# First block of a two-layer MLP behind gated attention: fp32 products from unsplit weights, decoding shared differently between VectorE and ScalarE, and weights loaded on the SyncE queue

## The chip, the cores and the metric

One core of a Trainium2 chip. The metric is the device time of one execution in microseconds (us). The kernel before takes 895.98 us (median of 3 runs, 895.06 to 896.11).

## The reference, cut to what matters

```
x = attn(q, k, v, f_logit)          # per head: state = f * state + k v^T ; y = q state
x = relu(x @ w_in) ** 2 @ w_out     # layer 0, 3072 tokens, 384 -> 2048 -> 384
out = elu(x @ w2_in) @ w2_out       # layer 1, same sizes
```

The weights arrive as 64-bit floats: each is two 32-bit words, and the kernel itself puts sign, exponent and mantissa together into a 32-bit float (it decodes them).

## The kernel before, in words

Tokens stand in 24 groups of 128 (g0 to g23); four groups make a block of 512 tokens, so there are six blocks per layer. The hidden size 2048 is cut into 16 slices of 128, numbered f. For a block i and a slice f, `up(i, f)` multiplies the block's input with the slice of w_in into a PSUM tile ph (9 matmuls: input and weights each split into a high and a low part in TensorE's reduced 32-bit format fp32r; products high-high, low-high, high-low). `between(i, f)` makes gg = relu(ph)^2 and its own parts gh and gl. `down(i, f)` multiplies with the slice of w_out into three PSUM tiles y (3 x 3 matmuls). The order is written out by hand: a table of steps (`START`) for the first four groups, then slots u = 2, 3, ...: the planned steps of the slot, up of unit u, down of unit u - 2, between of unit u. The first block is slots 0 to 17. In this text U3 is up(0, 3), D3 is down(0, 3), U1,0 is up(1, 0).

A weight slice f of layer 0 goes through these steps. `load_raw`: one DMA of 768 KB; slices 0 to 2 on SyncE's queue (SP), the others on ScalarE's. `decode`: one pass of ScalarE (L54) and three of VectorE (L56, L59, L60) over 128x768. `split`: the high part by ScalarE (L370), the low part by VectorE (L371). For f < 8 (`WHOLE`) only the w_in half is split then; the w_out half stays as it was decoded for the first block, whose D0 to D7 are done in plain fp32 (one matmul of two passes instead of three matmuls: 6 passes for a down), and `split_rest` splits it in slots 10 to 13.

Groups g4 to g7 are the attention of the second block and are worked in the slots of the first: load_qk, a_gate, a_decay (VectorE scans), a_scale, a_keys (transpose tp), a_near (TensorE), a_far, a_out (TensorE, tile o). Between a_far and a_out ScalarE makes `seen`, a small copy from o for which a_out waits. After a_out ScalarE copies o to x1 in four pieces (L293), and six small DMAs on SP (L296) move rows of x1 into place. Engines work through their own instructions in the order written, SP too: a DMA behind one that waits is not issued before it.

Of the kernel before, what the change touches and what calls it, by code (L numbers as in the profile page):

```python
# [32 lines left out]

START = """f0 q0 f1 I q1 M v0 f2 v1 f3 g0 q2 d0 q3 c0 g1 v2 d1 s0 r0 c1 r1 t0 g2 k0 m0 g3 s1 t1 y0 d2 c2 h0 v3 k1
# [4 lines left out]
NEAR = dict(zip(range(B, NG), (4, 6, 9, 11, 19, 21, 23, 25, *range(28, 4 * NG - 23, 4))))  # L39
ORDER = np.r_[64:128, 63:-1:-1]  # L40
# [21 lines left out]

def chunked(ctx, tc, ff, qk, vk, vz, wraw, mask, ident, flag, out):
# [79 lines left out]
    def a_gate(g):  # L143

        f = st[g]["ff"]
        A.activation(f, f, AF.Tanh, scale=0.5)
        if g < B:
            A.activation(f, f, AF.Copy, scale=0.5, bias=0.5)
        else:
            G.tensor_scalar(out=f, in0=f, scalar1=0.5, scalar2=0.5, op0=ALU.mult, op1=ALU.add)  # L150

    def a_decay(g):


        a, f = ds[g % 2], st[g]["ff"]
        V.memset(lim[:, ::65], 1.0)
        V.tensor_tensor_scan(out=a[:, 0, 0:520], data0=f[:, 0:520], data1=lim[:, 0:520], initial=1.0, op0=ALU.mult, op1=ALU.max)  # L157
        V.reciprocal(out=lim[:, 65::65], in_=a[:, 0, 64::65])
# [12 lines left out]

    def a_scale(g):

        a = ds[g % 2]
        for o, first, apart in ((0, 66, 456), (1, 0, 588)):
            y = st[g]["qk"[o]].rearrange("r (p h l) -> r p h l", h=2, l=64)
            z = bass.AP(a.tensor, a.offset + first, [a.ap[0], [130, NP], [apart, 2], [1, 64]])

            E = G if o == 0 and 0 < g < B else V
            E.tensor_tensor(out=y, in0=y, in1=z, op=ALU.mult)  # L180
# [173 lines left out]
    def whole(layer, f):  # L354
        return layer == 0 and f < WHOLE

    def decode_weights(layer, f):

        if whole(layer, f):
# [13 lines left out]
    def split_weights(layer, f):  # L373

        pool, tag = (two, "raw") if layer else (wpool, "w")
        t = pool.tile([128, 2, 2, DM], F32R, tag=tag, name=f"w{layer}_{f}")
        if layer == 0:
            wt[layer, f] = t
        if whole(layer, f):
            split(t[:, :, 0:1], raws[layer, f][:, :DM].bitcast(F32))  # L380
            return
# [1 line left out]
        if layer:
            nc.sync.dma_start(out=wst[f], in_=t.bitcast(F32))

    def split_rest(f):
        split(wt[0, f][:, :, 1:2], raws.pop((0, f))[:, DM:].bitcast(F32))

# [360 lines left out]
```

## Time and profile before

| | |
|---|---|
| median of 3 runs | 895.98 us |
| profiled execution: own time / span | 894.93 us / 893.0 us |
| busy: TensorE (PE) / VectorE (DVE) / ScalarE (ACT) / GpSimd (POOL) | 97% / 63% / 50% / 31% |
| chain that ended last: PE / DVE / DMA | 88% / 5% / 2% |
| granted TensorE clock, mean | 0.996 |

The span runs from the first to the last instruction; the rest of the execution's own time lies around it. Busy shares are means over stages with different limits: over the first 110 us VectorE is busy more than 90% of most stretches, afterwards TensorE is.

### The profile page before, as it was taken

What the parts mean: (1) busy time and instruction counts of PE and PEld (TensorE: products, weight loads), DVE (VectorE), ACT (ScalarE), POOL (GpSimd) and SP (SyncE); (2) the same over time, 40 slices, a digit from 0 to 9 for tenths busy, and PEclk for the clock granted to TensorE, in tenths of its full rate; (3) what the DMA queues carried; (4) which work ended last, traced back from release to release, by engine and by line L of the source; (5) the groups of instructions that cost most, each with busy time, mean ns of one, the idle gap of its engine ahead of it and who ended that gap; (6) DMA issues with size and microseconds to landing.
All of it is one profiled execution on the core that took longest, in us unless ns stands there. A gap on an engine that the chain in (4) does not pass through costs nothing.

```text
span 893.0 us, 15986 instructions
## 1 busy us (share of the span) xinstructions
PE 867.9 (97%) x6273; PEld 704.3 (79%) x6273; DVE 564.8 (63%) x858; ACT 443.6 (50%) x797; POOL 279.9 (31%) x245
## 2 busy tenths in 40 slices
PE   6699999999999999999999999999999999999997
PEld 4555778888888888888888888888888888888886
DVE  8799987778777877844331565564555555655543
ACT  4456863545555445544544444544444544544443
POOL 3101036343333332323333232323232323333331
PEclk9999999999999999999999999999999999999999
DMA  9555342324354433523587400100100100100001
GB/s 268 190 167 186 121 118 74 113 87 151 129 160 153 162 114 116 181 87 109 183 310 249 166 12 1 60 12 1 60 13 0 60 12 1 60 12 11 26 1 39
DMA packets 34210, 88.66 MB, mean 99 GB/s; under 512 B 5552, under 2 KB 11056, under 8 KB 34128
## 3 DMA queue, kind: packets, MB, share of 16 engines
q1 hardware_dynamic: 32112, 77.22, 26.6%
q10 hardware_dynamic: 2016, 10.36, 3.4%
q8 instruction: 50, 0.82, 0.4%
q14 instruction: 32, 0.26, 0.1%
HBM read 64.55 MB, written 22.02 MB: 97 GB/s over the span
## 4 chain that ended last, share of the span: by engine, by line
PE 88%; DVE 5%; DMA 2%; ACT 1%; issue 1%; SPq 1%; POOL 0%; ACTq 0%; DVEq 0%
PE ph L413 42%; PE y L477 41%; DMA ff<-ff 1%; PE o L270 1%; PE o L285 1%; PE tp L186 1%; DVE ds L157 1%; PE sk_a L209 1%; SPq L296 1%; DVE dec L59 1%; DVE w L371 1%; PE sk_a L218 1%; DVE pair L60 0%; DVE pair L59 0%; DMA vk<-vk 0%
## 5 line engine op out<-in xcount | busy, mean ns | idle before, releaser
L460 POOL TENSOR_TENSOR gl<-gg,gh 128x512 fp32r<-128x512 f32 x175 | 234.4, 1340 | 457.1 <-PE ph L413 189.5
L477 PE MATMUL y<-gh,wf 128*128 128x512 f32 (+1 forms) x582 | 177.8, 387 | 0.0
L446 DVE SCALAR_TENSOR_TENSOR t<-r,t 128x512 f32<-128x512 f32 (+1 forms) x97 | 71.4, 736 | 154.5 <-ACT r L445 154.2
L477 PE MATMUL y<-gh,w 128*128 128x512 f32 x528 | 162.5, 389 | 0.0
L413 PE MATMUL ph<-xh,w 128*128 128x512 f32 x576 | 155.1, 403 | 4.6 <-ACT w L370 3.8
L442 ACT ACTIVATE r<-ph 128x512 f32<-128x512 f32 (+1 forms) x97 | 57.8, 596 | 181.5 <-PE ph L413 176.6
L413 PE MATMUL ph<-xh,wf 128*128 128x512 f32 (+1 forms) x582 | 146.4, 387 | 0.0
L413 PEld LDWEIGHTS ph<-xh,w 128*128 128x128 f32 x576 | 105.1, 189 | 29.6 <-ACT w L370 4.2
L477 PEld LDWEIGHTS y<-gh,wf 128*128 128x128 f32 x582 | 108.8, 188 | 22.3
L413 PEld LDWEIGHTS ph<-xh,wf 128*128 128x128 f32 x582 | 108.6, 188 | 22.3
L477 PEld LDWEIGHTS y<-gh,w 128*128 128x128 f32 x528 | 99.1, 188 | 20.6
L477 PE MATMUL y<-gl,wf 128*128 128x512 f32 (+1 forms) x291 | 112.6, 387 | 0.0
L477 PE MATMUL y<-gl,w 128*128 128x512 f32 x264 | 102.7, 389 | 0.0
L434 ACT ACTIVATE r<-ph 128x512 f32<-128x512 f32 x88 | 52.2, 593 | 95.7 <-PE ph L413 87.4
L413 PE MATMUL ph<-xl,w 128*128 128x512 f32 x288 | 81.3, 390 | 1.0 <-DVE xl L322 1.0
L413 PE MATMUL ph<-xl,wf 128*128 128x512 f32 (+1 forms) x291 | 81.1, 387 | 0.0
L440 DVE TENSOR_TENSOR gh<-r 128x512 fp32r<-128x512 f32 x64 | 44.0, 688 | 54.9 <-ACT r L434 51.2
L447 DVE SCALAR_TENSOR_TENSOR gg<-ph,t 128x512 f32<-128x512 f32 (+1 forms) x97 | 66.6, 687 | 10.4 <-DVE t L446 0.5
L413 PEld LDWEIGHTS ph<-xl,w 128*128 128x128 f32 x288 | 54.3, 189 | 13.1 <-DVE xl L322 1.4
L477 PEld LDWEIGHTS y<-gl,wf 128*128 128x128 f32 x291 | 54.6, 188 | 11.1
L413 PEld LDWEIGHTS ph<-xl,wf 128*128 128x128 f32 x291 | 54.4, 188 | 11.1
L444 ACT ACTIVATE t<-r 128x512 f32<-128x512 f32 (+1 forms) x97 | 61.0, 629 | 3.1
(101 smaller groups left out, 1013.9 us busy)
## 6 DMA issues: line engine op xcount, KB each, us to landing
raw<-wraw SPq DMA_DIRECT2D x19, 768.0 KB, 6.3
wst<-w SPq DMA_DIRECT2D x16, 768.0 KB, 4.3
wf<-wst SPq DMA_DIRECT2D x16, 768.0 KB, 5.2
raw<-wraw ACTq DMA_DIRECT2D x13, 768.0 KB, 4.3
ff<-ff SPq DMA_DIRECT2D x22, 227.9 KB, 4.5
k<-qk SPq DMA_DIRECT2D x22, 224.0 KB, 4.4
q<-qk SPq DMA_DIRECT2D x22, 224.0 KB, 4.8
x2d<-yo SPq DMA_DIRECT2D x18, 256.0 KB, 2.9
```

The costliest lines, as they stand in the source:

```text
L59: V.scalar_tensor_tensor(out=out, in0=hi, scalar=0x80000000, in1=out, op0=ALU.bitwise_and, op1=ALU.bitwise_or)
L157: V.tensor_tensor_scan(out=a[:, 0, 0:520], data0=f[:, 0:520], data1=lim[:, 0:520], initial=1.0, op0=ALU.mult, op1=ALU.max)
L186: PE.transpose(tp[:, p, 0:ROWS], k[:, p], idt[:ROWS, :ROWS])
L413: PE.matmul(ph, w[:, a, 0, 128 * k:128 * k + 128], b[:, k, c], start=(m == 0), stop=(m == len(todo) - 1))
L434: A.activation(r[:, c], ph, AF.Relu)
L440: V.tensor_tensor(out=gh[:, c], in0=r[:, c], in1=r[:, c], op=ALU.mult)
L442: A.activation(r[:, c], ph, AF.Relu, scale=-1.0)
L444: A.activation(t[:, c], r[:, c], AF.Tanh, scale=-0.5)
L446: V.scalar_tensor_tensor(out=t[:, c], in0=r[:, c], scalar=1.0, in1=t[:, c], op0=ALU.add, op1=ALU.mult)
L447: V.scalar_tensor_tensor(out=gg[:, c], in0=ph, scalar=0.0, in1=t[:, c], op0=ALU.max, op1=ALU.add)
L460: G.tensor_tensor(out=gl, in0=gg, in1=gh, op=ALU.subtract)
L477: PE.matmul(yp_[i][m][:, c], w[:, 128 * m:128 * m + 128], b[:, c], start=(f == 0 and n_ == 0), stop=(f == NF - 1 and n_ == 2), skip_group_ ...
```

## The change: what it does

- The raw weights of layer 0 are all loaded on SP's queue. Slices 2 to 9 go to buffers of the large pool `wpool` and are loaded four slots ahead (before: three, in two buffers); slices 10 to 15 three slots ahead, in the two old buffers.
- Decoding is divided into `begin` (two ScalarE passes: the old one, and one that reads a byte of each weight and writes the three low bits as a word) and `finish` (two VectorE passes; L56 is gone).
- U0 to U2 are done in plain fp32, with an unsplit copy `x` of the block's input (`a_whole`, four small ScalarE copies). All of D0 to D15 are done in plain fp32. `between` of the first block makes neither gh nor gl.
- `store_weights` copies the decoded half (for f < 3 the whole slice) by a DMA on SP into the slice's final tile; `split_rest` splits it there in place in slots 14 to 31.
- a_scale of g3 multiplies q on VectorE, not GpSimd; gate and first scan of g0 are done in two halves; `START` and four places of the attention (`NEAR`) are rearranged: a_near of g4 and g5 is in slots 5 and 7 (before 4 and 6).

```diff
-START = """... t1 y0 d2 c2 h0 v3 k1
-m1 s2 d3 v4 t2 y1 c3 k2 m2 s3 h1 w0 t3 l0 y2 k3 m3 W0 r2 h2 q4 w1 y3 f4 l1
-l2 h3 l3 W1 g4 r3 w2 U0 B0 L0 W2 d4 U1 B1 L1 w3 r4 T f5"""
+START = """... t1 y0 d2 c2
+x0 r2 k1 m1 s2 d3 f4 q4 t2 y1 c3 b0 k2 s3 m2 x1 r3 t3 b1 y2 x2 m3 y3 k3 w0 h0 h1 r4 x3 w1 U0 B0 b2 C0 w2 h2 h3
+g4 C1 l0 l1 U1 B1 b3 l2 l3 w3 b4 C2 r5 f5 T"""
-WHOLE = 8
-NEAR = dict(zip(range(B, NG), (4, 6, 9, 11, 19, ...
+DIRECT = 3
+EARLY = 10
+NEAR = dict(zip(range(B, NG), (5, 7, 9, 11, 19, ...
+def begin(nc, raw, out):
+    words = raw.bitcast(U32).rearrange("p (n two) -> p n two", two=2)
+    top = raw.bitcast(U8).rearrange("p (n b) -> p n b", b=8)[:, :, 3]
+    hi, lo = words[:, :, 1], words[:, :, 0]
+    nc.scalar.activation(out.bitcast(F32), hi.bitcast(F32), AF.Copy, scale=2.0**-112)
+    nc.scalar.activation(lo, top, AF.Copy, scale=1 / 32, bias=-31 / 64)
+def finish(nc, raw, out):
+    ...
+    V.scalar_tensor_tensor(out=out, in0=out, scalar=3, in1=lo, op0=ALU.logical_shift_left, op1=ALU.bitwise_or)
+    V.scalar_tensor_tensor(out=out, in0=hi, scalar=0x80000000, in1=out, op0=ALU.bitwise_and, op1=ALU.bitwise_or)
+    def a_whole(g):
+        if g == 0:
+            st["x"] = wpool.tile([128, NK, 512], F32, tag="w", name="x")
+        A.activation(st["x"][:, :, 128 * g:128 * g + 128], st[g]["yp"], AF.Copy)
     def load_raw(layer, f):
-        raws[layer, f] = raw = two.tile([128, 2 * DM], I64, tag="raw", name=f"raw{layer}_{f}")
-        (nc.sync if layer or f < 3 else nc.scalar).dma_start(out=raw, in_=wraw[layer, f])
+        pool, tag = (wpool, "w") if layer == 0 and 1 < f < EARLY else (two, "raw")
+        raws[layer, f] = raw = pool.tile([128, 2 * DM], I64, tag=tag, name=f"raw{layer}_{f}")
+        nc.sync.dma_start(out=raw, in_=wraw[layer, f])
+    def store_weights(f):
+        wt[0, f] = t = wpool.tile([128, 2, 2, DM], F32R, tag="w", name=f"w0_{f}")
+        t, b = t.bitcast(F32), decs[f].bitcast(F32)
+        if f < DIRECT:
+            nc.sync.dma_start(out=t[:, 1].rearrange("r i m -> r (i m)"), in_=b)
+        else:
+            nc.sync.dma_start(out=t[:, 1, 1], in_=b[:, DM:])
+    def split_up(f):
+        split(wt[0, f][:, :, 0:1], decs.pop(f)[:, :DM].bitcast(F32))
+    def split_rest(f):
+        t = wt[0, f] if f < DIRECT else wt[0, f][:, :, 1:2]
+        split(t, t[:, 1].rearrange("r i m -> r (i m)").bitcast(F32))
     def up(i, f):
+        if i == 0 and f < DIRECT:
+            ...
+            for k in range(NK):
+                PE.matmul(ph, w[:, 128 * k:128 * k + 128], st["x"][:, k], start=k == 0, stop=k == NK - 1)
     def between(i, f):
-        if i == 0 and f < WHOLE:
+        if i == 0:
     def down(i, f):
-            terms = (raws[0, f][:, DM:].bitcast(F32), gg),
+            terms = (wt[0, f][:, 1, 1].bitcast(F32), gg),
     for f in range(NF):
-        at(f - 3, load_raw, 0, f)
-        at(f - 2, decode_weights, 0, f)
-        at(f - 1, split_weights, 0, f)
-        if f < WHOLE:
-            at(10 + f // 2, split_rest, f)
+        at(f - 1, store_weights, f)
+        if f >= DIRECT:
+            at(f - 1, split_up, f)
+    for f in range(NF):
+        at(f - 3 if f >= EARLY else f - 4, load_raw, 0, f)
+        at(f - 2 if f >= EARLY else f - 3, begin_weights, f)
+        at(f - 2, finish_weights, f)
+        at(f + (NF - 2 if f < DIRECT else NF), split_rest, f)
```

In the order listings below, a row is line, operation, output<-inputs, size; xN counts equal rows that follow each other. SP's queue of before, from the loads of g6 to the copies x1_5 of g5:

```order
L126 DMA k6_614<-qk 112x512
L127 DMA q6_613<-qk 112x512
L296 DMA x1_4_716<-x1_4_716 16x128 x6
L114 DMA ff7_740<-ff 112x521
L140 DMA vk6_771<-vk 128x384
L126 DMA k7_774<-qk 112x512
L127 DMA q7_773<-qk 112x512
L296 DMA x1_5_927<-x1_5_927 16x128 x6
```

The same stretch of SP's queue in the changed kernel (raw0_10 is the raw slice 10 of layer 0, w0_8 the store of slice 8):

```order
L320 DMA x1_4_747<-x1_4_747 16x128 x6
L147 DMA k7_766<-qk 112x512
L148 DMA q7_765<-qk 112x512
L408 DMA w0_8_771<-pair8_614 128x384
L383 DMA raw0_10_777<-wraw 128x768
L161 DMA vk6_803<-vk 128x384
L408 DMA w0_9_813<-pair8_614 128x384
L383 DMA raw0_11_822<-wraw 128x768
L320 DMA x1_5_912<-x1_5_912 16x128 x6
L408 DMA w0_10_930<-dec0_10_817 128x384
L383 DMA raw0_12_939<-wraw 128x768
```

The raw loads of slices 10 and 12 now stand behind the six copies of x1_4 and of x1_5. ScalarE's order of before, slots 7 to 9:

```order
L352 DMA raw0_10_787<-wraw 128x768
L422 ACTIVATE r0_7_802<-ph0_7_0_789 128x512
L423 ACTIVATE gg0_7_803<-r0_7_802 128x512
L231 ACTIVATE kt6_811<-tp6_806 128x448
L370 ACTIVATE w0_9_821<-dec0_9_782 128x768
L54 ACTIVATE dec0_10_824<-raw0_10_787 128x768
L352 DMA raw0_11_829<-wraw 128x768
L434 ACTIVATE r0_8_846<-ph0_8_0_831 128x512
L435 ACTIVATE gg0_8_847<-r0_8_846 128x512
L438 ACTIVATE gh0_8_844<-r0_8_846 128x512
L316 ACTIVATE xh1_852<-x1_4_716 128x3x128
L277 ACTIVATE seen5_874<-o5_0_856 48x4
```

The same slots of ScalarE in the changed kernel:

```order
L474 ACTIVATE r0_7_792<-ph0_7_0_779 128x512
L475 ACTIVATE gg0_7_793<-r0_7_792 128x512
L255 ACTIVATE kt6_801<-tp6_796 128x448
L425 ACTIVATE w0_9_813<-pair8_614 128x384
L70 ACTIVATE dec0_10_817<-raw0_10_777 128x768
L72 ACTIVATE raw0_10_777<-raw0_10_777 128x768
L474 ACTIVATE r0_8_837<-ph0_8_0_824 128x512
L475 ACTIVATE gg0_8_838<-r0_8_837 128x512
L301 ACTIVATE seen5_859<-o5_0_841 48x4
```

The raw loads are gone from ScalarE's queue, the decoding of slice 10 is two passes, and seen5 still stands behind it.

## Rows read from the trace of the kernel before

**Rows 1.** Windows: us, then busy of each engine, PEclk, DMA share, GB/s.

```profile
40.00:41.00 1.00, 1.00 (x3) 0.83 (x3) 0.93 (x1) 0.77 (x2) 0.00 (x0) 0.50 0.02 6
...
90.00:100.00 10.00, 9.71 (x160) 7.91 (x161) 9.79 (x18) 7.83 (x18) 0.00 (x0) 1.00 0.39 120
...
160.00:180.00 20.00, 20.00 (x212) 16.42 (x210) 14.14 (x22) 10.11 (x22) 9.64 (x9) 1.00 0.44 133
```

**Rows 2.** Timeline of TensorE: start us, us, what, count, idle before and releaser.

```profile
30.00 1.65 PE L413 MATMUL ph<-xh,w 128*128 128x512 f32 x6 [0.58 <-ACT xh L316]
...
39.41 3.09 PE L413 MATMUL ph<-xh,w 128*128 128x512 f32 x6 [3.77 <-ACT w L370]
...
63.84 0.66 PE L270 MATMUL o<-q,s 48*48 48x64 f32 x32
...
65.80 1.65 PE L413 MATMUL ph<-xh,w 128*128 128x512 f32 x6
...
78.23 2.74 PE L477 MATMUL y<-gg,pair 128*128 128x512 f32 x6
80.90 0.66 PE L270 MATMUL o<-q,s 48*48 48x64 f32 x32
...
120.76 1.52 PE L413 MATMUL ph<-xh,w 128*128 128x512 f32 x6
...
124.84 1.52 PE L413 MATMUL ph<-xh,w 128*128 128x512 f32 x6
...
128.92 0.55 PE L186 MATMUL tp<-idt,k 112*128 112x112 f32 x4
```

**Rows 3.** Timeline of VectorE, same columns.

```profile
26.51 1.33 DVE L236 COPY_PREDICATED ss<-msk,sc 128x512 f32<-128x512 int32 x2
...
49.74 0.07 DVE L156 MEMSET lim<- 112x9 f32 x1
...
52.64 0.55 DVE L371 TENSOR_TENSOR w<-pair,w 128x384 fp32r<-128x384 f32 x1
53.11 0.55 DVE L56 TENSOR_SCALAR pair<-pair 128x768 uint32<-128x768 uint32 x1
53.70 0.96 DVE L59 SCALAR_TENSOR_TENSOR pair<-raw,pair 128x768 uint32<-128x768 uint32 x1
...
55.57 0.43 DVE L236 COPY_PREDICATED sd<-tri,sk_a 128x256 f32<-128x256 int32 x1
...
57.29 0.68 DVE L180 TENSOR_TENSOR q<-q,ds 112x512 f32<-112x512 f32 x1
```

**Rows 4.** Timeline of ScalarE, same columns.

```profile
46.11 0.90 ACT L54 ACTIVATE pair<-raw 128x768 f32<-128x768 f32 x1
46.91 0.59 ACT L422 ACTIVATE r<-ph 128x512 f32<-128x512 f32 x1
47.52 0.64 ACT L423 ACTIVATE gg<-r 128x512 f32<-128x512 f32 x1
48.06 0.53 ACT L231 ACTIVATE kt<-tp 128x448 f32<-128x448 f32 x1
...
95.61 0.23 ACT L277 ACTIVATE seen<-o 48x4 f32<-48x4 f32 x2
96.59 0.79 ACT L293 ACTIVATE x<-o 48x256 f32<-48x256 f32 x2 [0.75 <-PE o L285]
```

**Rows 5.** Timeline of SP's queue, same columns (SPq: issue of a DMA).

```profile
66.74 3.85 SPq L296 DMA_DIRECT2D x<-x  x6
70.70 0.51 SPq L114 DMA_DIRECT2D ff<-ff  x1
```

**Rows 6.** DMA issues: count, KB, us to landing; window 73:75, then the whole run.

```profile
raw<-wraw ACTq DMA_DIRECT2D x1, 768.0 KB, 5.4
...
raw<-wraw ACTq DMA_DIRECT2D x13, 768.0 KB, 4.3
```

**Rows 7.** Waits, window 0:145: engine and line, for whom, us in total, times, longest.

```profile
PE o L285 <- ACT seen L277: 1.7, 3, 1.2
```

**Rows 8.** Waits of SP's queue, window 0:130, same columns.

```profile
SPq L296 <- ACT x L293: 36.6, 7, 12.7
```

More of the change, by code (lines that the diff above doesn't have):

```diff
@@ L15 @@
 U32 = mybir.dt.uint32
+U8 = mybir.dt.uint8
 I64 = mybir.dt.int64
@@ L31 @@
 BLOCKS = [(layer, sum(n[:i]), n[i]) for layer, n in enumerate(SIZES) for i in range(len(n))]
[L34 to L36 removed]
+START = """f0 q0 f1 I q1 M f2 v0 f3 v1 g0 q2 d0 q3 c0 g1 r0 d1 s0 v2 c1 v3 t0 g2 k0 m0 g3 r1 s1 t1 y0 d2 c2
+x0 r2 k1 m1 s2 d3 f4 q4 t2 y1 c3 b0 k2 s3 m2 x1 r3 t3 b1 y2 x2 m3 y3 k3 w0 h0 h1 r4 x3 w1 U0 B0 b2 C0 w2 h2 h3
+g4 C1 l0 l1 U1 B1 b3 l2 l3 w3 b4 C2 r5 f5 T"""
 STAGED = 27
[L38 to L39 removed]
+DIRECT = 3
+EARLY = 10
+NEAR = dict(zip(range(B, NG), (5, 7, 9, 11, 19, 21, 23, 25, *range(28, 4 * NG - 23, 4))))
 ORDER = np.r_[64:128, 63:-1:-1]
@@ L60, in decode @@
     V.scalar_tensor_tensor(out=out, in0=lo, scalar=29, in1=out, op0=ALU.logical_shift_right, op1=ALU.bitwise_or)
+def begin(nc, raw, out):
[5 more added lines that the diff above has]
+def finish(nc, raw, out):
+    words = raw.bitcast(U32).rearrange("p (n two) -> p n two", two=2)
+    hi, lo = words[:, :, 1], words[:, :, 0]
+    V = nc.vector
+    V.scalar_tensor_tensor(out=out, in0=out, scalar=3, in1=lo, op0=ALU.logical_shift_left, op1=ALU.bitwise_or)
+    V.scalar_tensor_tensor(out=out, in0=hi, scalar=0x80000000, in1=out, op0=ALU.bitwise_and, op1=ALU.bitwise_or)
 def chunked(ctx, tc, ff, qk, vk, vz, wraw, mask, ident, flag, out):
@@ L145, in a_gate @@
         f = st[g]["ff"]
-        A.activation(f, f, AF.Tanh, scale=0.5)
         if g < B:
-            A.activation(f, f, AF.Copy, scale=0.5, bias=0.5)
+            for c in (slice(0, 260), slice(260, 521)) if g == 0 else (slice(0, 521),):
+                A.activation(f[:, c], f[:, c], AF.Tanh, scale=0.5)
+                A.activation(f[:, c], f[:, c], AF.Copy, scale=0.5, bias=0.5)
         else:
+            A.activation(f, f, AF.Tanh, scale=0.5)
             G.tensor_scalar(out=f, in0=f, scalar1=0.5, scalar2=0.5, op0=ALU.mult, op1=ALU.add)
@@ L156, in a_decay @@
         V.memset(lim[:, ::65], 1.0)
-        V.tensor_tensor_scan(out=a[:, 0, 0:520], data0=f[:, 0:520], data1=lim[:, 0:520], initial=1.0, op0=ALU.mult, op1=ALU.max)
+        for c in (slice(0, 260), slice(260, 520)) if g == 0 else (slice(0, 520),):
+            V.tensor_tensor_scan(out=a[:, 0, c], data0=f[:, c], data1=lim[:, c], initial=1.0, op0=ALU.mult, op1=ALU.max)
         V.reciprocal(out=lim[:, 65::65], in_=a[:, 0, 64::65])
@@ L177, in a_scale @@
             z = bass.AP(a.tensor, a.offset + first, [a.ap[0], [130, NP], [apart, 2], [1, 64]])
-            E = G if o == 0 and 0 < g < B else V
+            E = G if o == 0 and 0 < g < B - 1 else V
             E.tensor_tensor(out=y, in0=y, in1=z, op=ALU.mult)
@@ L350, in load_raw, with begin_weights @@
     def load_raw(layer, f):
-        raws[layer, f] = raw = two.tile([128, 2 * DM], I64, tag="raw", name=f"raw{layer}_{f}")
-        (nc.sync if layer or f < 3 else nc.scalar).dma_start(out=raw, in_=wraw[layer, f])
[L354 to L359, printed above, removed]
+        pool, tag = (wpool, "w") if layer == 0 and 1 < f < EARLY else (two, "raw")
+        raws[layer, f] = raw = pool.tile([128, 2 * DM], I64, tag=tag, name=f"raw{layer}_{f}")
+        nc.sync.dma_start(out=raw, in_=wraw[layer, f])
+    decs = {}
+    def begin_weights(f):
+        if f < EARLY:
             if f % 2 == 0:
@@ L363, in decode_weights, with finish_weights @@
         else:
-            b = two.tile([128, 2 * DM], U32, tag="dec", name=f"dec{layer}_{f}")
+            b = two.tile([128, 2 * DM], U32, tag="dec", name=f"dec0_{f}")
+        begin(nc, raws[0, f], b)
+        decs[f] = b
+    def finish_weights(f):
+        finish(nc, raws.pop((0, f)), decs[f])
+    def store_weights(f):
[10 more added lines that the diff above has]
+        split(t, t[:, 1].rearrange("r i m -> r (i m)").bitcast(F32))
+    def decode_weights(layer, f):
+        b = two.tile([128, 2 * DM], U32, tag="dec", name=f"dec{layer}_{f}")
         decode(nc, raws[layer, f], b)
@@ L373, in split_weights @@
     def split_weights(layer, f):
[L375 to L381, printed above, removed]
+        t = two.tile([128, 2, 2, DM], F32R, tag="raw", name=f"w{layer}_{f}")
         split(t, raws.pop((layer, f)).bitcast(F32))
[L383 to L387, printed above, removed]
+        nc.sync.dma_start(out=wst[f], in_=t.bitcast(F32))
     def fetch_weights(f):
@@ L404, in up @@
         layer, t0, n = BLOCKS[i]
+        if i == 0 and f < DIRECT:
+            ph = ps_h.tile([128, n], F32, tag="h", name=f"ph{i}_{f}_0")
+            w = decs[f].bitcast(F32)
+            for k in range(NK):
+                PE.matmul(ph, w[:, 128 * k:128 * k + 128], st["x"][:, k], start=k == 0, stop=k == NK - 1)
+            hs[i, f] = [ph]
+            return
         xh, xl = xr[i]
@@ L478, in down @@
                         yp_[i][m][:, c], w[:, 128 * m:128 * m + 128], b[:, c],
-                        start=(f == 0 and n_ == 0), stop=(f == NF - 1 and n_ == 2),
+                        start=(f == 0 and n_ == 0), stop=(f == NF - 1 and n_ == len(terms) - 1),
                         skip_group_check=i == final[0],
```

8 lines of the change are left out of this document (4 added, 4 removed).

## Prediction

> **What bounds the kernel now.** I read the windows first. In 160 to 180 us TensorE (PE) is busy 20.00 of 20 us and VectorE 14.14 [rows 1], and so it stays to the end: after the first block a microsecond comes off the total only if it comes off TensorE. In 90 to 100 us VectorE is busy 9.79 of 10 [rows 1]. So the first block is the place, and the timeline of TensorE gives its two ends: U0 starts at 30.00, and the last down of the block is over when the transpose at 128.92 starts [rows 2]. All that the change does is priced by what it does to 128.92; the profiled execution's own time is 894.93 us, 1.05 below the median of 895.98.
>
> What is in these 98.9 us? An up and a down of nine fp32r matmuls take 124.84 - 120.76 = 4.08 us, 2.04 each; a down in fp32 takes 2.74 with the tail of its last pass, and 2.67 to the next start [rows 2]: I use 2.6. One far-near-out part of the attention takes 65.80 - 63.84 = 1.96 [rows 2]. With 18 ups at 2.04 (some 0.15 more where one follows attention), 8 downs at 2.6, 8 at 2.04 and some 9.8 us of attention, TensorE has 85 us of work there, and waits for the rest, about 14.
>
> **What goes from VectorE.** L56 is 53.70 - 53.11 = 0.59 [rows 3], 16 times: 9.4 us. Eight subtractions gl of 128x512 go (about 0.6 each, as L180 of that size [rows 3]): 4.8. The low parts of 16 half slices and of three more are moved behind the block, 0.47 each [rows 3]: 8.9. That is 23 us of about 86. What is left per slice is finish, 55.57 - 53.70 = 1.87, and one split, 0.47 [rows 3]. Over two slots, with the scans of one group (52.64 - 49.74 = 2.90), its masks and states (57.29 - 55.57 = 1.72) and q and k (1.2), VectorE has 10.5 us [rows 3], TensorE 2 x (2.04 + 2.6) and about 2.6 of attention, 11.9. So from the fourth slice on VectorE no longer sets the pace.
>
> **What comes to TensorE.** Eight downs and three ups go from 2.04 to 2.6: 11 x 0.56 = 6.2 us, all on the path where nothing waits. An up in fp32 is not in the trace; its passes are those of the fp32 down, between 2.04 and 2.67, so 2.6.
>
> **What comes to ScalarE.** The second pass of begin is not in the trace. Nearest is L54, same 768 columns at the same stride: 46.91 - 46.11 = 0.80 from start to start [rows 4]. Below it lies 0.6 (L422, 512 columns [rows 4]); nothing rules out twice 0.80, if reading bytes or writing words that far apart is slow. I take 0.80, so begin is 1.6. ScalarE's sum over two slots is then 9.6 of 11.9 us (begin 3.2, two high parts 0.9, r and gg 2.3, gate, kt and xh 1.4, seen and x1 1.8); it is not the sum that hurts but the order, below.
>
> **What is hidden.** The stores land long before they are read (three slots, over 13 us, against 4.3 us for a load of four times the size [rows 6]). The late splits (16 in slots 14 to 31, 13 at 0.47 on VectorE and 3 at about 0.9) come to 8.8 us in some 85 us in which VectorE has 30% free [rows 1]: nothing, at most 2 us where they meet scans.
>
> **The walk.** I follow the changed order with these durations.
>
> U0: the masks of group 3 stood behind the first decoding (26.51 [rows 3]) and no longer do, some 1.6 us gained; but ScalarE now makes state, two xh and the last x in front of U0, about 1.1 more. U0 at 29.5, between 28.5 and 30.5 (30.00 before).
>
> U2: begin of slice 2 stands behind r and gg of U0 on ScalarE. U0 ends at 32.2, r and gg take 48.06 - 46.91 = 1.15 [rows 4], begin 1.6, finish 1.87: U2 starts at 36.8. U1 is over at 34.7, TensorE waits 2.1.
>
> U3: VectorE does four xl (0.47 each, as the split) to 38.7, waits for begin of slice 3 (35.0 + xh, gate, r, gg, begin = 39.25), finish to 41.1, then the scans of g4, 2.9, and only then the split: 44.5. TensorE is through U2 and D0 at 42.0 and waits 2.2 in U3, over at 46.4.
>
> Then D1, tp, U4, D2, near, U5, D3, tp, U6, D4, far-near-out: 4 x 2.6, 3 x 2.2 (an up behind attention is some 0.15 longer), two tp at 0.4, near 1.1, 2.0 = 20.9. The attention of g4 is out at 67.3. All slices up to 9 are ready by then.
>
> Slice 10: its raw load stands on SP behind the six copies of x1_4, k7, q7 and a store. ScalarE makes the first two pieces of x1_4 in 0.79 [rows 4], the copies take 3.85, the other issues 0.5 each [rows 5]: issued at 67.3 + 0.8 + 3.85 + 1.5 = 73.45. Slice 10 of before, with loads in flight ahead of it, took 5.4 [rows 6]: landed at 78.85. On ScalarE begin stands in front of r, gg and seen5, and out5 waits for seen5 (such waits are there before: 1.7 us, three times [rows 7]). 78.85 + 1.6 + 1.15 + 0.23 + out 0.5 = 82.35. TensorE is ready for out5 at 78.8: it waits 3.05.
>
> From here it is a loop: x1 0.79, copies 3.85, store 0.5, load 4.3 (median [rows 6]), begin 1.6, r and gg 1.15, seen 0.23, out 0.5: 12.9 us from out5 to out6 and again to out7, against 12.0 and 10.55 of TensorE's own work (U9, D7, tp, U10, D8, attention; U11, D9, U12, D10, far and out). Waits 0.9 and 2.35; out7 ends at 108.15. Behind it stand U13, U14, U15, U1,0, U1,1 and D11 to D15: 2.2 + 4 x 2.04 + 5 x 2.6 = 23.4, so the block ends at 131.5, against 128.92: **2.6 us later**. By the own time 897.5; with the 1.05 us between own time and median, **898.6 us**. In sum: 6.2 of work more on TensorE, waits of 10.6 instead of some 14, and a start 0.5 earlier.
>
> **A rule that would change this.** The issue times above come to little, and SP's x copies did wait before: 36.6 us for ScalarE, up to 12.7 at a time [rows 8]. The Trainium skill (DMA: Bandwidth & Descriptors, Issuing engines are not separate DMA queues) says that issuing DMAs from several engines only saves the time of issuing. By that rule the move of the raw loads from ScalarE's queue to SP costs nothing, which is the first rival below; the trace does not agree here, since what a load loses on SP is not issue time but the wait of what stands ahead of it [rows 8].
>
> **Rivals.**
> 1. Faster: the raw loads of 10, 12 and 14 never hold ScalarE, because SP passes the copies sooner than I reckon, or they land sooner. For: the before kernel issued its slice 10 from ScalarE between 73 and 75 us [rows 6], no earlier than the walk has it. Against: there ScalarE had 0.8 less to do behind the landing, and TensorE was a slot behind. If they don't hold it, the three waits of 3.05, 0.9 and 2.35 fall away: 125.2, 3.7 us earlier, 892.3. It decides from the place where raw 10 lands before 75.8 (73.45 would have to be 70.4): if so, this side.
> 2. No change: half of the waits come. Landing at 4.1 to 4.3 instead of 5.4 takes 1.1 off the first, a U0 at 28.5 takes another 1.0 off everything: 896.5, within 0.2% of before.
> 3. Slower still: the clock. After the gap of 3.77 us before U2 the granted clock was 0.50, the lower of the two levels (1.2 GHz), and six matmuls took 3.09 instead of 1.65 [rows 1, 2]. A gap of 2.1 (U2) and of 3.05 and 2.35 may do the same; at U2 the wait in U3 hides it, at out5 0.9 of 1.5 us is hidden, at out7 nothing: 2.1 more, 900.7. The second pass of begin at twice 0.80 adds 0.8 in three turns and in the two early chains: 4 us, 902.6.
>
> **How the numbers follow.** A measurement here tells about 0.2% (1.8 us) from no change. The walk as it stands, 896.8 to 900.5: 0.45. Rival 3: 0.09. Rival 2: 0.18. Rival 1: 0.28. With a small part of the walk's own spread inside 0.2%: slower 0.50, same 0.22, faster 0.28. For the range, the lower end goes down to rival 1's 892.3 and a little below (a U0 at 28.5 as well): 891.8; the upper end to the doubled pass, 902.2.
>
> **What would show it.** U0 near 29.5, gaps of about 2 us at U2 and in U3. ScalarE idle some 5 us for raw 10 (73.5 to 78.9) and 3 us or more for 12 and 14, while out5 to out7 wait for seen. VectorE below 90% busy after 70 us. The second pass of begin near 0.9 us long. Wrong is the forecast if out5 starts before 80 us, if out5 to out7 stand less than 12.3 us apart, or if the stretch behind 135 us is no longer one of TensorE without gaps.

## The result, and the profile after

The changed kernel takes 906.81 us (median of 4 runs, 906.0 to 907.86), the kernel before 896.03 us beside it: a ratio of 1.0124, with a 95% interval of 1.0106 to 1.0141. Slower was right; 898.6 us was forecast, and 906.81 lies above the whole range. The profiled execution takes 906.0 us, its span 904.2, against 894.93 and 893.0 before.

Where are the 11 us? The timeline of TensorE in the changed kernel says it with its last row: the transpose behind the first block starts at 139.50, where it stood at 128.92 [rows 2]. That is 10.6 of the 11.2 us between the spans.

```profile
29.63 5.42 PE L454 MATMUL ph<-x,pair 128*128 128x512 f32 x12 [1.56 <-ACT x L339]
37.46 2.81 PE L454 MATMUL ph<-x,pair 128*128 128x512 f32 x6 [2.41 <-DVE pair L81]
...
44.81 1.43 PE L465 MATMUL ph<-xh,w 128*128 128x512 f32 x5 [1.73 <-DVE w L426]
...
67.43 1.66 PE L465 MATMUL ph<-xh,w 128*128 128x512 f32 x6
...
77.33 0.66 PE L294 MATMUL o<-q,s 48*48 48x64 f32 x32
...
82.18 0.34 PE L242 MATMUL sk_a<-vk,kt 64*64 64x48 f32 x1 [3.71 <-DMA vk<-vk]
84.71 1.16 PE L309 MATMUL o<-sd,vk 64*48 64x64 f32 x32 [1.43 <-ACT seen L301]
85.80 2.93 PE L465 MATMUL ph<-xh,w 128*128 128x512 f32 x6
...
100.43 1.65 PE L465 MATMUL ph<-xh,w 128*128 128x512 f32 x6
...
113.98 0.72 PE L309 MATMUL o<-sd,vk 64*48 64x64 f32 x32 [3.41 <-ACT seen L301]
114.63 2.85 PE L465 MATMUL ph<-xh,w 128*128 128x512 f32 x6
117.28 1.25 PE L465 MATMUL ph<-xl,w 128*128 128x512 f32 x3
...
139.50 0.55 PE L210 MATMUL tp<-idt,k 112*128 112x112 f32 x4
```

Up to 77.33, where far5 starts (a_far of g5; out5 and near6 are a_out of g5 and a_near of g6), the changed kernel is on the forecast's times. Then TensorE waits 3.71 us for vk6 and 1.43 for seen5, out5 ends at 85.80, and behind it six matmuls of U9 take 2.93 us, where those behind out4 at 67.43 take 1.66. The wait for seen comes again before out7 (3.41), and there too the next six are slow (2.85).

The windows, same columns as [rows 1], show the same places: TensorE busy 6.39 of 10 us in 80 to 90 with a granted clock of 0.53 (close to the lower of its two levels, 1.2 GHz), and 6.59 in 110 to 120. VectorE, 9.79 of 10 us in 90 to 100 before, is busy 4.28: it has stopped being the bound, as forecast. At 160 to 180 TensorE is full again.

```profile
80.00:90.00 10.00, 6.39 (x74) 5.22 (x75) 5.53 (x11) 6.67 (x13) 0.00 (x0) 0.53 0.25 99
90.00:100.00 10.00, 9.87 (x134) 5.86 (x136) 4.28 (x6) 5.63 (x11) 0.00 (x0) 0.96 0.64 219
110.00:120.00 10.00, 6.59 (x77) 4.68 (x78) 3.93 (x5) 7.99 (x16) 0.00 (x0) 0.83 0.28 104
160.00:180.00 20.00, 20.00 (x330) 16.54 (x329) 13.98 (x27) 11.09 (x26) 9.04 (x7) 1.00 0.32 95
```

Who makes seen late? ScalarE's timeline: begin 10, 12 and 14 (L70, L72) wait 7.93, 2.26 and 4.13 us for their raw load, and seen5 comes 2.84 us behind the start of begin 10. The second pass of begin (L72) takes 83.22 - 82.44 = 0.78 from start to start; 0.80 was forecast.

```profile
81.65 0.89 ACT L70 ACTIVATE dec<-raw 128x768 f32<-128x768 f32 x1 [7.93 <-DMA raw<-wraw]
82.44 0.88 ACT L72 ACTIVATE raw<-raw 128x768 uint32<-128x768 uint8 x1
83.22 0.58 ACT L474 ACTIVATE r<-ph 128x512 f32<-128x512 f32 x1
...
84.49 0.23 ACT L301 ACTIVATE seen<-o 48x4 f32<-48x4 f32 x2
...
96.70 0.91 ACT L70 ACTIVATE dec<-raw 128x768 f32<-128x768 f32 x1 [2.26 <-DMA raw<-wraw]
...
110.93 0.89 ACT L70 ACTIVATE dec<-raw 128x768 f32<-128x768 f32 x1 [4.13 <-DMA raw<-wraw]
```

And who makes raw 10 late? SP's queue in the changed kernel (the rows of before are [rows 5]): behind the six copies of x1_4 come k7, q7 and store 8, then raw 10 at 74.31, vk6, store 9 and raw 11.

```profile
68.36 4.19 SPq L320 DMA_DIRECT2D x<-x  x6
72.66 0.51 SPq L147 DMA_DIRECT2D k<-qk  x1
73.23 0.41 SPq L148 DMA_DIRECT2D q<-qk  x1
73.74 0.52 SPq L408 DMA_DIRECT2D w<-pair  x1
74.31 0.58 SPq L383 DMA_DIRECT2D raw<-wraw  x1
74.98 0.42 SPq L161 DMA_DIRECT2D vk<-vk  x1
75.50 0.51 SPq L408 DMA_DIRECT2D w<-pair  x1
76.06 0.58 SPq L383 DMA_DIRECT2D raw<-wraw  x1
86.72 4.38 SPq L320 DMA_DIRECT2D x<-x  x6
91.20 0.54 SPq L408 DMA_DIRECT2D w<-dec  x1
91.78 0.59 SPq L383 DMA_DIRECT2D raw<-wraw  x1
```

The list of DMA issues, one transfer at a time (us to landing last; raw 10, then vk6, then raw 12): raw 10 took 7.3 us where the forecast took 5.4 [rows 6]. vk6, a quarter of the size and issued behind raw 10, lands with it.

```profile
raw<-wraw SPq DMA_DIRECT2D x1, 768.0 KB, 7.3
...
vk<-vk SPq DMA_DIRECT2D x1, 192.0 KB, 7.2
...
raw<-wraw SPq DMA_DIRECT2D x1, 768.0 KB, 4.8
```

### The profile page after: what moved, and what is told of

It is laid out like the page before. It is cut to its first block, busy times and chain, and to the rows that moved or that the text cites. A ratio compares the mean times of both kernels' runs of the same rounds, so it can differ in the third digit from the quotient of the medians.

```text
span 904.2 us, 15967 instructions
## 1 busy us (share of the span) xinstructions
PE 878.0 (97%) x6240; PEld 705.2 (78%) x6240; DVE 553.5 (61%) x841; ACT 454.3 (50%) x816; POOL 279.3 (31%) x244
## 4 chain that ended last, share of the span: by engine, by line
PE 91%; ACT 3%; DMA 2%; DVE 2%; issue 1%; SPq 0%; ACTq 0%; DVEq 0%
PE ph L465 42%; PE y L529 42%; DMA raw<-wraw 2%; PE o L309 1%; PE o L294 1%; PE tp L210 1%; PE yp L278 1%; PE sk_a L233 1%; PE sc L220 1%; ACT raw L72 1%; PE sk_a L242 1%; DVE ds L181 0%; DMA ff<-ff 0%; PE sk_h L242 0%; PE ph L454 0%
## 5 line engine op out<-in xcount | busy, mean ns | idle before, releaser
L465 PE MATMUL ph<-xh,w 128*128 128x512 f32 x558 | 152.1, 408 | 1.7 <-DVE w L426 1.7
L529 PE MATMUL y<-gh,w 128*128 128x512 f32 x480 | 147.8, 389 | 0.0
L465 PEld LDWEIGHTS ph<-xh,w 128*128 128x128 f32 x558 | 102.9, 191 | 26.2 <-DVE w L426 2.4
L529 PEld LDWEIGHTS y<-gh,w 128*128 128x128 f32 x480 | 90.1, 188 | 18.7
L486 ACT ACTIVATE r<-ph 128x512 f32<-128x512 f32 x80 | 47.6, 595 | 105.1 <-PE ph L465 88.5
L529 PE MATMUL y<-gl,w 128*128 128x512 f32 x240 | 93.4, 389 | 0.0
L497 ACT ACTIVATE r<-r 128x512 f32<-128x512 f32 (+1 forms) x97 | 60.9, 628 | 3.1
```

Source lines behind the costliest of these rows:

```text
L465: PE.matmul(ph, w[:, a, 0, 128 * k:128 * k + 128], b[:, k, c], start=(m == 0), stop=(m == len(todo) - 1))
L497: A.activation(r[:, c], r[:, c], AF.Exp, scale=-1.0)
L529: PE.matmul(yp_[i][m][:, c], w[:, 128 * m:128 * m + 128], b[:, c], start=(f == 0 and n_ == 0), stop=(f == NF - 1 and n_ == len(terms) - 1) ...
```

## The experiments

Theory A: the raw loads of slices 10 to 15 stand on SP behind the x1 copies and what follows them; ScalarE's begin waits for them ahead of seen, and out waits for seen. Rival B: the time goes into dearer fp32 passes, begin's second pass and the clock. All runs, each with the ratio to the kernel before on the same chip, and the first block's end in its profiled execution:

| run | median us | ratio to before, 95% | block ends |
|---|---|---|---|
| kernel before | 895.98 | | 128.92 |
| changed kernel | 906.81 | 1.0106 to 1.0141 | 139.50 |
| e1: raw 10 to 15 on ScalarE's queue | 896.29 | 0.9998 to 1.0017 | 129.24 |
| p1: before, all raw loads on SP | 900.06 | 1.0037 to 1.0071 | 132.22 |
| e2: on SP, ahead of the copies | 899.83 | 1.0027 to 1.0058 | 133.80 |
| e10: e2 and vk6, vk7 earlier | 894.05 | 0.9972 to 0.9990 | 127.16 |
| e4: vk6, vk7 earlier alone | 909.18 | 1.0144 to 1.0178 | 142.01 |
| b1: e1 and vk6, vk7 earlier | 893.66 | 0.9973 to 0.9992 | 127.87 |
| e5: raw 11 earlier | 908.43 | 1.0119 to 1.0159 | 143.17 |
| e6: raw 10, 12 and vk first behind the copies | 902.64 | 1.0064 to 1.0098 | 137.61 |
| e9: raw 10 and vk6 alone so | 902.62 | 1.0057 to 1.0085 | 136.79 |
| e3: begin behind seen | 904.96 | 1.0088 to 1.0123 | 138.42 |
| p2: begin in one pass for 10 to 15 | 904.87 | 1.0091 to 1.0131 | 136.77 |
| e7, e8: six, three needless matmuls before out7 | 906.86, 905.42 | 1.0115 to 1.0151, 1.0098 to 1.0133 | 140.04, 138.26 |
| b2: b1 and downs 8 to 15 in fp32r | 891.12 | 0.9941 to 0.9972 | 122.94 |
| b4: b2 and raw 8, 9 on ScalarE's queue | 891.97 | 0.9945 to 0.9974 | 123.83 |

### Which part: the raw loads (e1, p1)

e1 undoes one line of the change for six loads:

```diff
-        nc.sync.dma_start(out=raw, in_=wraw[layer, f])
+        (nc.sync if layer or f < EARLY else nc.scalar).dma_start(out=raw, in_=wraw[layer, f])
```

> The changed kernel, but the raw loads of slices 10 to 15 are issued from ScalarE's queue and no longer from SP's. Theory A (on SP these loads stand behind the six copies of x1, ScalarE's begin waits for them, and seen and out stand behind begin): raw 10 is issued at about 69 instead of 74.31 us, lands by 75, begin 10 waits for nothing, out5 to out7 wait less than 0.7 us each, the first block ends at 125.5 to 127 instead of 139.50, and the time falls from 906.8 to 892 to 894, under the kernel before. Rival B (the time is lost to the dearer fp32 passes on TensorE, to begin's second pass and to the clock): the waits for seen stay near 3 us and the time stays above 903.

896.29 us: 10.5 of the 10.8 us are gone by this line alone, and B falls as the cause of the loss, since every fp32 pass and every second pass is still there. (They aren't free: b2, below, takes eight of the dearer passes back and gains again.) A's size was missed by 2 to 4 us. The waits of e1's TensorE show what is left: vk6, issued on SP behind k7, q7 and store 8 and 1.15 us after raw 11 on ScalarE's queue, still lands 6.0 us after its issue.

```profile
PE sk_a L242 <- DMA vk<-vk: 2.0, 1, 2.0
...
PE ph L465 <- ACT r L474: 0.7, 1, 0.7
PE o L309 <- ACT seen L301: 0.3, 1, 0.3
```

p1 does that one part alone, in the kernel before: `(nc.sync if layer or f < 3 else nc.scalar)` becomes `nc.sync`.

> The kernel before with one part of the change alone: all raw loads of layer 0 are issued from SP, in the place in the order that they had on ScalarE. Theory A (the queue alone does the harm): the loads of 10, 12 and 14 stand behind the copies of x1 here too, ScalarE waits for them ahead of seen, and the first block ends 3 to 8 us later: 899 to 904. Rival P (it hurts only in a kernel whose TensorE and VectorE are a slot ahead; here VectorE is the bound and hides the late loads): 895 to 897.

900.06 us, in A's span: the block ends 3.3 us later (132.22), and the wait for seen7 grows from the 1.25 us of before to 2.58. So the move does harm by itself, with the old order around it: 4.6 us, but less than half of the 10.5 in the changed kernel. And only 3.3 us of it stand in the first block; 1.4 us of the rest lie behind TensorE's last row (7.75 us from there to the end of the span, 6.3 in the kernel before), a difference that comes again in b2 and b4 and stays open. At least two things differ in the changed kernel that may explain the larger loss there, and weren't tried apart: stores stand in the queue too, and VectorE is no longer late itself.

### The queue or the order in it (e2, e4, b1, e10)

e2 leaves all loads on SP and puts the planner's entries for them ahead of the attention's:

```diff
+    for f in range(EARLY, NF):
+        at(f - 3, load_raw, 0, f)
     for g in range(B, NG):
...
-        at(f - 3 if f >= EARLY else f - 4, load_raw, 0, f)
+        if f < EARLY:
+            at(f - 4, load_raw, 0, f)
```

> The changed kernel, but in each slot the raw load of slices 10 to 15 is issued on SP ahead of the copies of x1 and not behind them: the same queue, another order. Theory A (it is the order on SP): raw 10 is issued by 62 us, raw 12 and 14 as soon as their buffers come free and ahead of the copies; out5 to out7 hardly wait, 892 to 895. Rival Q (it is the one queue: all loads, stores and copies of SP share it and land later for that): raw loads still take 6 us and more to land, the waits for seen stay, above 900. Rival B: above 903.

899.83 us, between the two. The wait for seen is gone (0.5 us in all), as A says, but vk6, now behind raw 11, lands after 6.8 us and near6 waits 3.34 us for it, with U9 at the lower clock behind. (In the profiled execution U0 also starts 2 us late, at 31.63.) e4 moves only vk6 and vk7 in the changed kernel, b1 does so in e1:

```diff
-        at(d + 1 if g < B + 2 else max(d + 1, NEAR[g - 1] + 1), load_v, g)
+        at(NEAR[g - 1] if g in (B + 2, B + 3) else d + 1 if g < B + 2 else max(d + 1, NEAR[g - 1] + 1), load_v, g)
```

> The changed kernel, but vk6 and vk7 are loaded on SP ahead of raw 10 and raw 12 (one slot earlier), so that the near part of group 6 no longer waits 3.7 us for vk6. Theory A: out5 waits for seen5 until 84.7 us whatever near6 does, so nothing changes: 905.5 to 908. Rival V (the late vk is what opens the gap of TensorE before out5): out5 comes about 3 us earlier, 903 to 904.

> The changed kernel with raw 10 to 15 on ScalarE's queue and vk6 and vk7 loaded one slot earlier on SP. With the raw loads out of the way, the near part of group 6 waited 2.0 us for vk6, and that was TensorE's only long wait behind 60 us. Theory A: the wait goes and the block ends 2 us earlier than with the queue alone (896.3): 894 to 895. Rival: the 2 us come back as a wait for seen or for the split of slice 10, since begin 10 and its finish are done no earlier: 896 to 897.

e4 takes 909.18 us, slower than either side had it: the wait for vk6 goes and the one for seen5 grows to 6.01 us, so V falls; and raw 10 and 12, with one more transfer ahead of them, come later (raw 12 is issued at 92.95 and lands after 6.0 us, before at 91.78 after 4.8). In b1, where the raw loads aren't in that queue, the same edit gains: 893.66 us, under the kernel before. vk6 still takes 5.6 us there, with raw 11 issued 0.31 us after it on the other queue, where in e4 and e10 it takes 2.7 directly behind the copies; in b1 it is in time because it is issued at 73.84 and no longer at 75.91. e10 puts e2 and this edit together.

> The changed kernel, all raw loads on SP, but in each slot ahead of the copies of x1, and vk6 and vk7 ahead of k, q and the stores. Theory O (it is the order in the queue, not the queue): no wait for seen over 1 us, no wait for vk, as with ScalarE's queue and vk ahead (893.7): 893.5 to 896. Rival Q (loads on the one queue land later, 5 to 7 us, and raw 12 and 14 hold the copies behind them while they wait for their buffers): 897 or more.

894.05 us, in O's span, with all loads on SP: the same as with ScalarE's queue (893.66). TensorE's waits in e10:

```profile
PE ph L454 <- DVE pair L81: 2.4, 1, 2.4
PE ph L454 <- ACT x L339: 1.6, 1, 1.6
PE o L309 <- ACT seen L301: 1.2, 2, 0.7
```

Nothing is left of vk6, and 1.2 us of seen. So it is the order and not the queue that cost the time. Q's first half holds all the same: raw 10, 11 and 12 land in 5.8, 7.2 and 6.3 us on the one queue, and in 4.3, 5.1 and 4.1 on ScalarE's in b1. In e10 they are issued so early that begin waits 0.49 us for one of them and not at all for the others. The Trainium skill (DMA: Bandwidth & Descriptors, Issuing engines are not separate DMA queues) says that DMAs issued by several engines run on the same 16 engines and interleave; e10 beside b1 agrees, and so does e1, where raw 11 on ScalarE's queue and q7, store 8, vk6 and store 9 on SP's, issued from 74.76 to 76.55 us, all took 5.8 to 6.2 us to land.

### Why raw 10 took 7.3 us (e5, e6, e9)

First guess: raw 11, issued 1.75 us behind it, shares the engines with it. In e5 raw 11 is loaded two slots earlier (`at(6 if f == 11 else ...)`).

> The changed kernel, but raw 11 alone is loaded two slots earlier, ahead of raw 10 (its buffer has long been free), so that raw 10, issued at 74.3 us as before, no longer shares the DMA engines with a second load of 768 KB. Theory A with shared data paths: raw 10 lands in about 5 us instead of 7.3, seen5 and out5 come 2.3 us earlier, and the time is 904 to 905.5. Rival Q (the landing of 7.3 us comes from the queue, not from raw 11): raw 10 still lands in over 7 us, 906 to 908.

Wrong: raw 10 still takes 7.4 us, and the kernel 908.43, a little over Q's span. What stands behind a load on its own queue is not what delays it here. e6 takes away what stands ahead: raw 10 and vk6 come directly behind the copies, ahead of k7, q7 and store 8 (raw 12 and vk7 likewise).

```diff
+        if g in (B + 2, B + 3):
+            at(NEAR[g - 1], load_raw, 0, 2 * g - 2)
```

> The changed kernel, all raw loads on SP and still behind the copies of x1_4 and x1_5; only raw 10 and vk6 (and raw 12 and vk7) now stand ahead of k7, q7 and the stores that came between. Theory F (what is issued on one queue lands in turn: raw 10 had to wait for the 640 KB of k7, q7 and store 8 ahead of it, and landed 4.9 us after store 8): raw 10 is issued at 72.7, lands in 4.5 to 5.4 us instead of 7.3, vk6 with it, out5 ends at 81 to 82.5 (the 82.35 of the prediction) instead of 85.43, and the time is 902 to 904. Rival S (the transfers share the DMA engines whatever their order): raw 10 still takes over 6.5 us, out5 ends after 83.5, 905 and more.

902.64 us, in F's span, and raw 10 lands in 4.7 us:

```profile
raw<-wraw SPq DMA_DIRECT2D x1, 768.0 KB, 4.7
```

So F stands and S falls: in these rows a load lands behind the transfers issued before it on its queue (k7 and q7, now behind raw 10, take 6.0 and 6.4 us instead of 2.9 and 3.0). The Trainium skill (DMA: Bandwidth & Descriptors, Two DMAs through the same engine are not ordered) has descriptors of one queue start in order on each engine, which fits. out5 ended at 82.76, nearly the 82.35 of the prediction, but that is luck: out4 ended at 69.06, 1.8 us later than forecast, and from there to out5 it was 13.70 us for the forecast's 15.05. Yet only 4 us of 10.8 came back, and the turn from out5 to out6 grew, from 14.63 us (U9 to U11) to 15.70. ScalarE's timeline of e6 shows a new wait:

```profile
90.07 0.52 ACT L425 ACTIVATE w<-dec 128x384 fp32r<-128x384 f32 x1
94.72 0.89 ACT L70 ACTIVATE dec<-raw 128x768 f32<-128x768 f32 x1 [4.12 <-DMA w<-dec]
```

begin 12 writes the dec buffer that store 10 reads, and store 10, now behind raw 12, lands only at 94.65 (issued at 89.55, 5.1 us). e9 moves raw 10 and vk6 alone.

> The changed kernel with raw 10 and vk6 alone ahead of k7, q7 and store 8 on SP; raw 12 and vk7 stay behind store 10 as in the changed kernel. Theory D (raw 12 ahead of store 10 held begin 12, whose dec buffer is free only when store 10 has landed): out5 as in the run with both moved (82.7), from out5 to out6 14.0 to 14.7 us instead of 15.7, so the time is 901 to 902.3. Rival: the second turn is 15.7 us or longer again for another reason, 902.5 to 904.

The turn shrinks to 14.92, the next to 14.25 (14.83 in e6), and the waits of begin 12 and 14 are for raw again; but the time, 902.62, is that of e6. D is seen in the rows, at 0.8 us, and in the two profiled executions (904.53 and 903.57 us), but not in the medians; the turn is longer than 12.9 without it.

### ScalarE's order and begin's second pass (e3, p2)

In e3 begin and finish of 10 to 15 stand in slot f - 1, behind seen and x1.

> The changed kernel, all loads on SP as they are; only begin and finish of slices 10 to 15 stand one slot later, on ScalarE behind seen and x1 and no longer ahead of them. Theory A (raw 10 hurts because begin stands in front of seen on ScalarE): out5 waits for nothing but vk6, ends at 82.5 to 83.5, out6 and out7 no longer depend on raw 12 and raw 14, and ups 10, 12 and 14 wait about 1 us each for their split: 897.5 to 901.5. Rival B (work on TensorE, begin's second pass and the clock): 905 or more, since none of that is less.

904.96 us, over 3 us above A's span. ScalarE no longer waits for a raw load ahead of seen, and seen5 is made at 78.15; but near6 waits 4.08 us for vk6 (it lands after 7.5 us), and then begin, finish and split stand in one slot: ScalarE waits 2.02 us for VectorE's finish every time, and r, gg and the next seen behind it are late again. Rows of its ScalarE (VectorE's finish runs from 102.11 to 104.06 us, between the second row and the third):

```profile
100.37 0.91 ACT L70 ACTIVATE dec<-raw 128x768 f32<-128x768 f32 x1
101.19 0.89 ACT L72 ACTIVATE raw<-raw 128x768 uint32<-128x768 uint8 x1
104.09 0.52 ACT L425 ACTIVATE w<-dec 128x384 fp32r<-128x384 f32 x1 [2.02 <-DVE dec L81]
```

The move put one wait of the in-order engine in the place of another. e3 by itself would have spoken for B; e1 and e10, which leave B's work untouched, rule B out.

p2 lets VectorE cut out the low bits again for slices 10 to 15, in three steps.

> The changed kernel, but for slices 10 to 15 begin is the one pass of before (0.8 us on ScalarE) and the low bits are cut out again by VectorE (finish of three steps). In the changed kernel's trace begin 10, 12 and 14 stand between a landing and seen, 1.6 us each. Theory A (the chain raw, begin, r, gg, seen, out, copies, raw is what sets the pace of out5 to out7): 0.8 us less in each of three turns, 904 to 905. Rival T (TensorE's own work at the lower clock sets the pace between out5 and out7, and the chain only the first wait): 906 to 907, at most 0.8 us less.

904.87 us (902.98 to 907.44, wider than A's span). From out4 to out5 it is 17.52 us instead of 18.37, and the turns are 14.14 and 13.34 instead of 14.63 and 14.20: 2.2 us of the 2.4 that A asks of the three. out5 itself ends no earlier (85.99), because out4 ended 1.04 us later in this execution. Another 1.5 us came since the wait before out7, 2.52 us, left the clock alone: U13 to the block's end is 23.3 us. So the pass is on the chain, and that the total lies in A's span is partly luck: in the profiled execution the clock gave 1.5 us that A didn't count, and the late out4 took 1.0 back.

### The clock (e7, e8)

Needless fp32 matmuls, whose result nobody reads, fill the wait before out7: six in e7, three in e8.

```diff
+        if g == 2 * B - 1:
+            busy = ps_a.tile([128, 512], F32, tag="a2", name="busy")
+            for _ in range(3):
+                PE.matmul(busy, idt, sd[0].rearrange("r a p t -> r (a p t)"), start=True, stop=True)
```

> The changed kernel; only in TensorE's wait of 3.41 us in front of out7 six needless fp32 matmuls of 128x512 (0.46 us each, 2.7 us) are put, behind the last far part, whose result nobody reads. In the changed kernel U13 behind that wait ran at half the clock (2.85 us for six matmuls instead of 1.65). Theory K (the gap costs the clock behind it, and at out7 nothing hides that): U13 takes 1.65 again, the first block ends about 1.5 us earlier relative to out7, 905 to 905.6. Rival: the clock falls there all the same, or what it costs is hidden: 906.5 to 907.

I had the price wrong: an fp32 matmul of this size is two rows of the trace, 0.9 us, so six took 5.42 us and held out7 some 1.7 us beyond seen7. U13 ran at 1.66, and the total, 906.86, shows gain and loss cancelled.

> The changed kernel with three needless fp32 matmuls (2.7 us by the 5.42 that six took) in TensorE's wait in front of out7. Theory K (the gap costs the clock behind it, and nothing hides that at out7): U13 takes 1.65 us for its first six matmuls instead of 2.85, out7 to the end of the block is 1.5 us shorter, the time 905 to 905.6. Rival: the clock falls there all the same, or the gain is given back: 906.4 to 907.2.

905.42 us (904.5 to 908.4), in K's span, though the runs overlap with those of the changed kernel (906.0 to 907.86); what decides are the rows. TensorE in e8:

```profile
110.40 2.84 PE L302 MATMUL busy<-sd,idt 128*128 128x512 f32 x6
114.31 0.72 PE L313 MATMUL o<-sd,vk 64*48 64x64 f32 x32 [1.06 <-ACT seen L305]
114.96 1.65 PE L469 MATMUL ph<-xh,w 128*128 128x512 f32 x6
116.45 0.84 PE L469 MATMUL ph<-xl,w 128*128 128x512 f32 x3
```

U13 is back at 1.65 and 0.84, and the granted clock over 115 to 118 us is 1.00 where it was 0.50. From U13 to the end of the block it is 138.26 - 114.96 = 23.30 us; in the changed kernel 139.50 - 114.63 = 24.87. The clock behind out7 costs 1.57 us.

### A version that beats both (b2, b4)

b2 is b1 with slices 8 to 15 split whole again, without a store, and their downs in fp32r:

```diff
+ROUNDED = 8
     def split_up(f):
+        if f >= ROUNDED:
+            split(wt[0, f], decs.pop(f).bitcast(F32))
+            return
...
-        if i == 0:
+        if i == 0 and f < ROUNDED:
```

> The kernel with raw 10 to 15 on ScalarE's queue and vk6, vk7 loaded earlier (893.66), with downs 8 to 15 of the first block in fp32r again: their slices are split whole, no copy of them is stored, and gl is made by VectorE. This takes back eight of the eleven dearer passes: theory A, TensorE sets the pace behind 70 us there, so 8 x 0.56 = 4.5 us come off, and the waits for dec buffers until a store has landed (2.7 and 0.75 us on ScalarE) go too: 888.5 to 890. Rival: gh, gl and the wider splits (1.8 us per slice on VectorE, 0.4 on ScalarE) make these engines late again, 892 or more.

891.12 us, 0.43% under the kernel before (0.28 to 0.59), between the two spans. The block ends at 122.94, 4.9 us before b1's; 0.8 of that stands already at the end of out4 (67.77 for 68.60), ahead of everything that b2 changes on TensorE, so the edit is worth 4.1, close to the 8 x 0.56 = 4.5 of the downs. VectorE does come near its limit (9.83 of 10 us in 120 to 130) without giving it back. But the medians differ by only 2.5 us: in b2 7.8 us lie between TensorE's last row and the end of the span, in b1 6.1. In both only the last copy, the last stores and the program's end stand there; what takes 1.7 us longer in b2 and b4 (and 1.4 in p1) stays open.

> The same, with raw 8 and raw 9 too loaded from ScalarE's queue into the two buffers of the other raw tiles and begun one slot later. In the changed kernel ScalarE waited 1.8 us for raw 9 in front of seen4, and r, gg and out4 behind it waited up to 0.9 us. Theory A: raw 9 lands earlier, out4 waits for nothing, 0.5 to 1 us less than the kernel with downs 8 to 15 in fp32r alone. Rival: begin 8 and 9 a slot later bring the chain begin, finish, split closer to U8 and U9 and cost as much: no difference.

891.97 us, no difference. The wait before seen4 goes, but there was none of out4 in b2 to save.

## Why the prediction was wrong

**What held.** U0 at 29.63 (forecast 29.5), waits of 2.41 and 1.73 at U2 and U3 (2.1, 2.2), out4 over at 67.43 (67.3; so close by luck, for in the variants that are the same up to there it is over at 67.31 to 69.06), VectorE relieved, the second pass at 0.80, the late splits and stores hidden behind the block (20.00 of 20 us). The mechanism was the right one: raw 10, 12 and 14, behind the x1 copies on SP, hold begin, begin holds seen, seen holds out. e1 and e10 show it: without it nothing is lost.

**The step that failed** is the one on slice 10 and its loop: "issued at 67.3 + 0.8 + 3.85 + 1.5 = 73.45 ... landed at 78.85", and "12.9 us from out5 to out6 and again to out7". The block ended at 139.50 instead of 131.5, 8.0 us late, and by the rows this is where they are:

- out5 ends at 85.80 instead of 82.35, 3.4 us late: 0.9 in the issue (74.31), 1.9 in the landing (7.3 for 5.4), 0.6 in the rest of the chain. The 5.4 was that of a load on ScalarE's queue with nothing in flight ahead of it there; on SP 640 KB of k7, q7 and store 8 were. With these behind it, it was 4.7 (e6). The 0.6 is nearly all out5 itself: 1.09 us for the forecast's 0.5, where out6 took 0.65; the granted clock over 80 to 90 us was 0.53.
- The turns are 14.63 and 14.20 us instead of 12.9, 3.0 us together. Along the first: copies start after 0.92 (0.79), take 4.38 (3.85), store 10 0.68 (0.5), landing 4.92 (4.3), begin 1.60, r and gg 1.26 (1.15), seen 0.23, out 0.64 (0.5). Six of the eight terms lie over the row they were taken from, 1.7 us in all, and two make 1.15 of it: the landing, taken from ScalarE's queue, and the copies.
- The last stretch is 24.87 instead of 23.4, 1.5 us, by the lower clock at U13 (e8: 23.30). That was rival 3, which had its effect right and was held for an event apart, with 0.09; in truth it followed from the longer waits, and all three terms came together.

**The other rivals.** Rival 1 put its point of decision right (raw 10 landed before 75.8): where it does and vk6 comes early too (b1, e10), the kernel is 2 us faster than before, though not by the rival's 3.7. The doubled second pass didn't come. The range's upper end had been taken from it, and the landing got no end of its own, though the trace of before had a row for it, in its list of DMA issues: the raw loads that SP issued there (19 of 32, and 16 of these layer 1's) took 6.3 us in the median. The forecast read the line beside it, ScalarE's 4.3 [rows 6]. As an end of the range 6.3 would have served better (0.9 and twice 2.0 us more: 903.5, an estimate); as a price it would have been wrong too, for raw 10, 12 and 14 landed in 7.3, 4.9 and 5.0.

```profile
raw<-wraw SPq DMA_DIRECT2D x19, 768.0 KB, 6.3
```

**What was left out** is vk6: it too moved behind raw 10, landed with it and held near6 for 3.71 us. That changes nothing while seen5 is later still (e4), but it is 2.6 us of the medians once the raw loads are out of the way (e1 against b1; 1.4 us of the block's end).

**The rule of the Trainium skill** was set against the row on SP's waits [rows 8] as if one of the two must be wrong. Both hold: with the order put right the queue costs no time (e10), the place in it does.

## What to carry to other kernels

When a load moves to another engine's queue, write down everything that is issued ahead of it there, with sizes: it is late by what the queue waits for, and it lands behind those bytes, so a landing time from another queue is no price for it. What is in flight on other queues counts as well. A small transfer that someone waits for belongs ahead of a large one in the same queue. Where a chain closes on itself, what is missing in its terms comes back every turn.

## What the runs showed of the hardware that was not expected

- Landing time goes by what is ahead on the queue: vk of 192 KB landed in 2.7 us directly behind the copies (e4, e10), in 7.2 right behind raw 10; raw 10 in 4.7 first and 7.3 behind 640 KB, with or without 768 KB behind it (e5). It isn't the own queue alone: directly behind the copies vk took 5.6 in b1, with 768 KB issued 0.31 us later on ScalarE's queue.
- The length of a wait alone doesn't tell whether the clock falls: the 2.4 us in front of U2 are in every variant of the changed kernel, but its six rows took 2.81 us in most and 4.51 in e4, e9, e10 and b4 (granted clock 0.57 over 37.5 to 41.5 us in e10, 1.00 over 37.5 to 40 in the changed kernel); 2.52 before out7 (p2) cost nothing, 2.08 in e6 did (2.60 for six matmuls instead of 1.65).
